# Windowed attention and its gated feed-forward: a first mask part of 32 rows, ten trios in the written-out start-up instead of twelve, and a new table

## The chip, the cores and the metric

The kernel runs on one core of a Trainium2 chip. The metric is device time in microseconds (us). The time before is 901.32 us, the median of three runs (901.23 to 902.42).

Five engines take part, each with an instruction queue of its own that it works through in order: TensorE (PE in the profile, its weight loads PEld) multiplies and transposes into PSUM; VectorE (DVE) and ScalarE (ACT) work element by element; GpSimd (POOL) takes over one subtraction per trio in the later part; SyncE (SP) issues nearly all loads. ACT issues the stores.

## The reference

```python
scores = scale * q @ k.T                      # 8 batches, 8 heads, 576 positions, 64 dims
mask: heads 0-3: 0 <= rel < 32;  heads 4-7: 0 <= rel < 128 and rel % 4 == 0
attn = softmax(where(mask, scores, -1e9));  x = attn @ v    # x: 4608 tokens x 512
h = x @ w_in                                  # 512 x 2048
g = h * clip(h + 3, 0, 6) / 6
out = g @ w_out                               # 2048 x 512
```

## The kernel before, in words

**Attention in trios.** Attention is cut into 48 trios, six per batch: four heads (kind 0 are the heads with the plain window, kind 1 those with the dilated one, whose positions are reordered by residue) times a third of the positions. One trio is 12 blocks of 32 queries for each of two pairs of heads. `block(ts, tv)` (line 262) issues the 48 small score products of trio `ts` and the 48 small value products of trio `tv`, interleaved; either may be left out. The first NFIRST = 12 trios ("masked", line 266) get their mask on PE: line 269 multiplies a unit matrix with the mask columns into the PSUM bank before the scores are added to it. Later trios get it on DVE, by an addition at line 221 in `largest`.

A trio's chain is: scores on PE; `largest` (line 215, a reduction) and `shifted` (line 227, a subtraction) on DVE; `exponent` (line 237) on ACT; a transpose; values on PE; `normalise` (line 240, three DVE instructions); a transpose back; then `high` (line 353, ACT rounds to fp32r) and `low` (line 360, the rest of it), which write the columns of `xh` and `xl` that the feed-forward reads. The first trios are transposed on PE, with a copy from PSUM by ACT (`turn_e`, `turned_e`, `turn_x`, `turned_x`, lines 292 to 315). The later ones go through `turn_by_blocks` (line 317): two transposes of 32 by 32 blocks on DVE, then four DMAs of 24 KB on SP. Their low part is made on POOL (`st_split`, line 367).

**Feed-forward in steps.** The tokens are 12 chunks of 384, the hidden width 16 slices of 128: 192 steps. Step n has a first product G (`gemm1`, line 448: 12 matmuls of 384 columns), the gate (`relu` on ACT, `gate` on DVE, `gate_high` on ACT, `gate_low` on DVE, lines 463 to 476), and a second product H (`gemm2`, line 478: nine matmuls of 512 columns, kept in three PSUM banks over a chunk). Every product is done in three parts, high by high, high by low, low by high. The list `steps` (line 374) starts with LEAD = 2 slices of chunk 0, then alternates between chunks 0 and 1, since each weight slice is fresh; from chunk 2 on it goes chunk by chunk. G of a chunk reads all trios that wrote its tokens: chunk 0 needs trios 0 to 4, chunk 1 trios 5 to 9 and earlier ones, chunk 2 (steps 32 on) trios 10 and 11 too.

**Weights.** Each of the 32 weight parts (two per slice) is loaded as 64-bit floats and converted: `U` and `Q` on ACT, `s`, `j`, `a` on DVE, `h` on ACT, `l` on DVE (lines 403 to 442).

**Order.** The start-up is written out in the table ORDER (line 40). Each word is an operation and a number, and every engine takes its own instructions in the order of the words. `k`, `v`, `w`, `M` load keys and queries, values, a weight part, a part of the mask; `B` is a block of scores with the values of trio number minus FOLLOW (3), `V` values alone; `R`, `S`, `X` are largest, shifted, exponent; `E`, `CA` the transpose and its copy; `Z` normalise; `Y`, `CX` the transpose back and its copy; `XH`, `XL` high and low part (on DVE here); `G`, `RE`, `T`, `GH`, `GL`, `H` the step. A word such as `k6@S2` is a load that SP issues only after S2 has ended. The old table holds 28 steps.

Behind the table, `step_at` (line 547) writes a step as G, the gate, what `beside` holds for its first half, H of two steps earlier (LAG), what `beside` holds for its second half. `place(p, ...)` (line 535) puts a part of a later trio at half-step p, counted from the start of chunk 2 (step 32), so that p = -1 is the second half of step 31. PE's order is this program order; DVE, ACT, SP and POOL are ordered by a scheduler there, in which a gate ranks above what lies beside its step. A trio takes four places: values of it and scores of the next at p, the transpose back at p + 1, the next one's transpose at p + 2, the split at p + 4. Below, "B10" and "V10" of a late trio mean its scores or values alone, and "G32" the G of step 32.

**Mask.** `mi` (line 125) holds a 128 by 128 unit matrix and the mask's six 384-column patterns; each pattern's 32 rows are repeated four times over the 128 partitions (`_mask`, line 597). It is loaded in two parts by columns (`load_mask`, line 502), and behind the first DVE copies the unit matrix to fp32 for the transposes (line 506).

Of the kernel before, what the change touches and what calls it, by code (L numbers as in the profile page):

```python
# [49 lines left out]
RE25 a5 s11 h5 T25 l5 w14@T20 G11 GH20 j11 GH25 a23 Q3 a11 h23 G6 Q14 l23 h11 U14 l11 w25@h5 U15 s14 H7 j14 Q25 s15  # L50
a14 H8 j15 RE11 RE6 T11 h14 T6 a15 H13 GH11 GL20 h15 l14 w2@U15 GH6 l15 w18@H8 Q2 G12 U2 GL25 GL11 U3 GL6 Q18 s2 s3
G17 U18 j2 RE12 j3 U19 T12 H20 a2 RE17 a3 h2 T17 h3 l2 H2 GH17 l3 w6@h15 GH12 Q6 s19 s18 U6 j19 G5 GL12 GL17 s6 a19
G1 RE5 j6 h19 T5 a6 GH5 H17 l19 w7@l15 Q7 h6 j18 U7 l6 w16@h19 H12 s7 RE1 GL5 Q16 T1 U16 j7 GH1 G9 s16 U17 GL1 a7
# [625 lines left out]
```

## Time and profile before

| | |
|---|---|
| runs | 901.23, 901.32, 902.42 us |
| the profiled execution | 901.94 us, of which 900.2 us are the span of the trace |
| PE busy | 881.0 us (98%) |
| PEld, DVE, ACT, POOL busy | 788.8, 450.0, 346.2, 43.3 us |
| start of the first step (G8) | 44.62 us |
| granted clock | full, but for two stretches between 22 and 34 us |

Matmuls are pipelined: the duration of one (0.34 us for 384 columns) is longer than the distance from one start to the next (0.17), and a group of instructions is best timed from its first start to the next group's first start. An idle time in square brackets at the end of a row is the engine's idle time just before the instruction, with what ended it; "issue" means that nothing in the profile accounts for it. [...]

### The profile page before, as it was taken

The numbers are of one execution on the slowest core, as the hardware profiler recorded it, in microseconds if no ns is written. First come the engines' busy times: TensorE is split into PE (matmuls) and PEld (weight loads), VectorE is DVE, ScalarE is ACT, GpSimd is POOL, SyncE is SP. The second block draws the span as 40 slices with busy tenths as digits, with TensorE's granted clock in tenths as the row PEclk, the third lists the DMA queues.
The fourth block names the chain that finished last, engine by engine and source line by source line (L and its number), as shares of the span: only waits on it lengthen the run. The fifth ranks groups of instructions, "written<-read, shape, count | busy, mean of one in ns | idle before, by whom it ended". The sixth has DMA issues, their size and how long they took to land.

```text
span 900.2 us, 20593 instructions
## 1 busy us (share of the span) xinstructions
PE 881.0 (98%) x8732; PEld 788.8 (88%) x8732; DVE 450.0 (50%) x952; ACT 346.2 (38%) x661; POOL 43.3 (5%) x59
## 2 busy tenths in 40 slices
...
DMA packets 37819, 74.86 MB, mean 83 GB/s; under 512 B 7264, under 2 KB 16608, under 8 KB 37728
## 3 DMA queue, kind: packets, MB, share of 16 engines
...
## 4 chain that ended last, share of the span: by engine, by line
PE 94%; DMA 2%; SPq 1%; ACT 1%; issue 1%; DVE 1%; ACTq 0%; DVEq 0%
PE ps_o L489 15%; PE ps_h L457 15%; PE ps_h L459 14%; PE ps_h L458 14%; PE ps_o L491 14%; PE ps_o L490 14%; PE ps_a L210 3%; PE ps_a L192 2%; PE ps_a L202 1%; PE ps_a L295 1%; DMA mi<-in_mask 1%; SPq L329 1%; DMA a<-a_t 1%; DMA first<-in_v 1%; ACT a L308 0%
## 5 line engine op out<-in xcount | busy, mean ns | idle before, releaser
L457 PE MATMUL ps_h<-xh,wt 128*128 128x384 f32 x768 | 260.6, 339 | 0.0
L468 DVE SCALAR_TENSOR_TENSOR t<-t,ps_h 128x384 f32<-128x384 f32 x192 | 106.1, 554 | 307.4 <-ACT t L465 307.2
L459 PE MATMUL ps_h<-xh,wt 128*128 128x384 f32 x768 | 258.5, 337 | 0.0
L458 PE MATMUL ps_h<-xl,wt 128*128 128x384 f32 x768 | 258.5, 337 | 0.0
L489 PE MATMUL ps_o<-wt,gh 128*128 128x512 f32 x576 | 228.4, 397 | 0.0
L491 PE MATMUL ps_o<-wt,gl 128*128 128x512 f32 x576 | 224.9, 390 | 0.0
L490 PE MATMUL ps_o<-wt,gh 128*128 128x512 f32 x576 | 224.4, 390 | 0.0
L465 ACT ACTIVATE t<-ps_h,three 128x384 f32<-128x384 f32 x192 | 110.8, 578 | 277.8 <-PE ps_h L459 271.9
L476 DVE TENSOR_TENSOR gl<-t,gh 128x384 fp32r<-128x384 f32 x192 | 106.5, 558 | 100.3 <-ACT gh L472 98.6
L457 PEld LDWEIGHTS ps_h<-xh,wt 128*128 128x128 f32 x768 | 144.6, 188 | 7.3
L458 PEld LDWEIGHTS ps_h<-xl,wt 128*128 128x128 f32 x768 | 144.7, 188 | 6.7
L459 PEld LDWEIGHTS ps_h<-xh,wt 128*128 128x128 f32 x768 | 144.7, 188 | 0.0
L472 ACT CAST gh<-t 128x384 fp32r<-128x384 f32 x192 | 98.0, 513 | 101.2 <-DVE t L468 97.3
L491 PEld LDWEIGHTS ps_o<-wt,gl 128*128 128x128 f32 x576 | 108.1, 188 | 23.2
L489 PEld LDWEIGHTS ps_o<-wt,gh 128*128 128x128 f32 x576 | 108.2, 188 | 18.4
L490 PEld LDWEIGHTS ps_o<-wt,gh 128*128 128x128 f32 x576 | 108.3, 188 | 15.9
L362 POOL TENSOR_TENSOR xl<-xf,xh 128x384 fp32r<-128x384 f32 (+3 forms) x54 | 43.0, 806 | 746.9 <-ACT xh L357 714.0
L238 ACT ACTIVATE e<-e 128x384 f32<-128x384 f32 x48 | 25.2, 525 | 105.7 <-DVE e L229 105.7
L192 PE MATMUL ps_a<-kq 64*32 64x64 f32 x1872 | 46.7, 226 | 0.0
L357 ACT CAST xh<-xf 128x384 fp32r<-128x384 f32 (+3 forms) x72 | 33.7, 535 | 32.4 <-DMA xf<-xf_t 32.2
L210 PEld LDWEIGHTS ps_a<-v,a 64*32 64x32 f32 x1728 | 35.8, 105 | 10.9 <-issue 9.2
L210 PE MATMUL ps_a<-v,a 64*32 64x65 f32 x1728 | 42.1, 225 | 1.0 <-DMA a<-a_t 1.0
...
## 6 DMA issues: line engine op xcount, KB each, us to landing
...
kq<-in_qk SPq DMA_DIRECT2D x39, 416.0 KB, 4.6
...
first<-in_qk SPq DMA_DIRECT2D x9, 416.0 KB, 5.3
...
```

The costliest lines, as they stand in the source:

```text
L192: return nc.tensor.matmul(ps[at : at + QB, 2 * QB * i : 2 * QB * (i + 1)], lhsT=x[rows, KW + QB * n : KW + QB * (n + 1)], rhs=x[rows, QB * ...
L210: return nc.tensor.matmul(ps[at : at + QB, i * W : (i + 1) * W], lhsT=ats[t][rows, QB * n : QB * (n + 1)], rhs=vs[t][rows, n, :], start=Tr ...
L457: nc.tensor.matmul(ph, lhsT=wt[f][:, 0, ks], rhs=a, start=(kt == 0), stop=False)
L458: nc.tensor.matmul(ph, lhsT=wt[f][:, 0, ks], rhs=b, start=False, stop=False)
L459: ins = nc.tensor.matmul(ph, lhsT=wt[f][:, 1, ks], rhs=a, start=False, stop=(kt == NK - 1))
L465: return nc.scalar.activation(ts[n], phs[n], AF.Relu, bias=three, scale=1.0)
L468: return nc.vector.scalar_tensor_tensor(out=ts[n], in0=ts[n], scalar=6.0, in1=phs.pop(n), op0=ALU.min, op1=ALU.mult)
L472: return nc.scalar.copy(ghs[n], ts[n])
L476: return nc.vector.tensor_tensor(out=gls[n], in0=ts.pop(n), in1=ghs[n].bitcast(F32), op=ALU.subtract)
L489: nc.tensor.matmul(po[c][tt], lhsT=gh[:, rows], rhs=wt[f][:, 2], start=first, stop=False)
L490: nc.tensor.matmul(po[c][tt], lhsT=gh[:, rows], rhs=wt[f][:, 3], start=False, stop=False)
L491: ins = nc.tensor.matmul(po[c][tt], lhsT=gl[:, rows], rhs=wt[f][:, 2], start=False, stop=(f == NF - 1))
```

## The change

The mask table gets a second unit matrix: a 32 by 32 one, repeated four times side by side (and on all four groups of rows). A product of its first 32 rows with the first 32 rows of a mask pattern repeats the pattern on all 128 partitions of PSUM. So line 269 now reads 32 partitions of the mask only, and the load is cut differently: M0 is rows 0 to 31 with all columns, M1 the unit matrix of the other 96 rows (256 bytes each), M2 the mask of these rows, which only the late trios read. The copy of the unit matrix to fp32 follows when M0 and M1 are both issued.

Ten trios instead of twelve stand in the table. Trios 10 and 11 become late ones: their scores at half-steps -10 and -9, transposes one half-step later, values at -7 and -5 (trio 12's scores with the latter), transposes back at -6 and -4, splits at -3 and -1; trio 12's own transpose stays behind, at -3. FOLLOW becomes a dictionary: seven blocks carry values, three trios' values go alone. LEAD = 6 puts six slices of chunk 0 ahead. The output scaling and the stores leave `gemm2` for a function of their own, `store`, with the word `O`. The table is new as a whole and has 27 steps, G20 first; most of its loads are let out by an `@`.

```diff
-LEAD = 2
-NFIRST = 12
+LEAD = 6
+NFIRST = 10
+NLATE = 12
-FOLLOW = 3
+FOLLOW = {2: 0, 3: 1, 4: 2, 5: 3, 7: 5, 8: 6, 9: 7}
 ORDER = """
-k2 k0 v0 M0 k9 M1 k4 k3 k1 w4 B0 R0 B2 S0 X0 E0 R2 CA0 v3@R2 S2 B3 X2 k6@S2 v6@X2 E2 Z0 B1 Q4 v2@E2 CA2 R3 U4 S3
-v1@R3 s4 X3 w10@s4 j4 Y0 R1 E3 CX0 k5@Y0 a4 CA3 XH0 S1 B6 v5@CA3 h4 XL0 X1 l4 v9@XL0 E1 w0@B6 Z3 CA1 R6 B4 S6 Q10 X6
-Y3 Z1 U10 B5 k7@Y3 CX3 R4 XH3 s10 S4 XL3 X4 j10 Y1 a10 E4 w1@B5 CX1 E6 Z2 CA4 XH1 R5 Y2 CA6 XL1 U0 B9 v4@CA6 S5 CX2
-s0 Q0 k11@CX2 j0 XH2 X5 Z6 v10@XH2 Q1 E5 XL2 h10 Y6 CA5 R9 CX6 k8@CA5 B7 a0 U1 S9 v8@a0 XH6 l10 X9 v7@XH6 XL6 h0 E9
-Z4 CA9 k10@E9 V9 R7 l0 Y4 B8 Z9 CX4 XH4 S7 s1 X7 XL4 Y9 Z5 w23@B8 E7 CX9 G8 CA7 R8 XH9 j1 XL9 Y5 RE8 S8 B10 w15@XL9
-CX5 a1 X8 w22@CX5 T8 XH5 E8 h1 Z7 G0 CA8 v11@h1 GH8 XL5 Q23 R10 w8@XL5 GL8 Y7 RE0 S10 B11 w29@Y7 CX7 l1 X10 T0 XH7
...
+k0 k1 M0 k2 k3 M1 w4 v0 v1 v3 B1 B0 R1 S1 R0 X1 S0 E1 X0 CA1 E0 w28@E0 Q4 CA0 U4 B2 k4@CA0 s4 j4 w26@s4 B3 R2 Z0
+v2@j4 S2 a4 X2 Q28 h4 k5@Q28 E2 U28 l4 Y0 CA2 v5@U28 R3 CX0 Z1 Q26 XH0 S3 Y1 U26 XL0 X3 s26 CX1 B4 s28 XH1 j26
+v4@s28 XL1 E3 a26 w2@XL1 CA3 R4 h26 B5 Z2 S4 k6@Z2 l26 X4 Y2 v6@S4 j28 E4 CX2 Z3 w0@E4 CA4 XH2 V4 R5 Q2 XL2 k7@XH2
+Y3 U2 Z4 CX3 v7@U2 B6 XH3 S5 s2 X5 Y4 XL3 k9@s2 E5 CX4 R6 XH4 j2 CA5 XL4 Q0 B7 k8@CA5 S6 U0 a2 X6 v8@U0 s0 E6 h2 Z5
+G20 w31@s0 CA6 R7 l2 S7 Y5 RE20 B8 j0 CX5 T20 X7 a0 XH5 E7 w1@X7 GH20 a28 G1 h0 XL5 CA7 Z6 h28 Q31 R8 B9 v9@Q31 RE1
+l0 Q1 S8 U1 GL20 Y6 G0 R9 X8 CX6 Z7 w6@R9 XH6 S9 XL6 Y7 X9 w3@G0 E8 T1 RE0 E9 s1 CX7 G2 T0 CA9 w27@CX7 j1 XH7 CA8
+l28 GH0 XL7 V9 GH1 RE2 a1 V8 Q3 Z9 h1 G22 w18@Q3 Z8 U3 Q6 l1 U6 GL0 Y9 Q27 w7@G22 s3 Y8 CX9 GL1 H0 CX8 j3 XH9 T2 XH8
+XL9 w9@XH9 GH2 XL8 RE22 a3 Q18 G7 Q7 GL2 T22 h3 w14@Q7 s6 U18 l3 G9 GH22 j6 RE7 Q9 GL22 U7 T7 a6 U27 H1 GH7 s18 s7
...
+w19@a10 Q8 a11 U8 T19 H18 h11 s8 GH19 l11 RE24 GL19 Q19 T24 G17 U19 j8 GH24 s19 U9 a8 H19 j19 h8 RE17 GL24 l8
+w20@l11 Q20 a19 U20 G4 T17 h19 s20 GH17 l19 j20 w21@l19 H12 RE4 GL17 a20 T4 h20 H17 s9 GH4 l20 GL4 Q21 j9 U21 G26 a9
+s21 h9 j21 G5 l9 w22@l20 RE26 a21 Q22 U22 T26 h21 s22 H4 GH26 l21 RE5 GL26 w23@l21 k10 k11 k12 v10 v11 v12 M2 T5 G14
+j22 GH5 GL5 a22 h22 H5 RE14 l22 Q23 T14 U23 G16 GH14 s23 GL14 j23 a23 H14 RE16 h23 T16 l23 GH16 G15 GL16 H16 RE15
+T15 GH15 G23 GL15 H24 RE23 T23 GH23 H15 GL23 O24 H23
 """
@@ -123,7 +123,8 @@
     xl = const.tile([P, NK, 2 * S], F32R, name="xl")
     mi = const.tile([P, mask.shape[1]], BF16, name="mi")
     ident_b = mi[:, :P]
-    mask_sb = mi[:, P:].rearrange("p (t x) -> p t x", t=6)
+    spread = mi[:QB, P : 2 * P]
+    mask_sb = mi[:, 2 * P :].rearrange("p (t x) -> p t x", t=6)
     ident = const.tile([P, P], F32, name="ident")
     three = const.tile([P, 1], F32, name="three")
@@ -266,7 +267,7 @@
         masked = ts is not None and ts < NFIRST
         if masked:
             _, kind, part = trios[ts]
-            nc.tensor.matmul(ps[:, :CH], lhsT=ident_b, rhs=mask_sb[:, 3 * kind + part], start=True, stop=False)
+            nc.tensor.matmul(ps[:, :CH], lhsT=spread, rhs=mask_sb[:QB, 3 * kind + part], start=True, stop=False)
         for i, u, r in blocks():
             if tv is not None:
                 product = (mm_values_first if tv < NFIRST else mm_values)(tv, pv, i, u, r)
@@ -482,27 +483,37 @@
         first = c not in po
         if first:
             po[c] = [ps_a.tile([P, DM], F32, name="ps_o", tag="ps_a") for _ in range(TT)]
-        if f == NF - 1:
-            o = wpool.tile([P, TT, DM], F32, name="o", tag="w")
         for tt in range(TT):
             rows = slice(tt * P, (tt + 1) * P)
             nc.tensor.matmul(po[c][tt], lhsT=gh[:, rows], rhs=wt[f][:, 2], start=first, stop=False)
             nc.tensor.matmul(po[c][tt], lhsT=gh[:, rows], rhs=wt[f][:, 3], start=False, stop=False)
             ins = nc.tensor.matmul(po[c][tt], lhsT=gl[:, rows], rhs=wt[f][:, 2], start=False, stop=(f == NF - 1))
-            if f == NF - 1:
+        done.add(n)
+        return ins
+    def store(n):
+        c, f = steps[n]
+        if f == NF - 1:
+            o = wpool.tile([P, TT, DM], F32, name="o", tag="w")
+            for tt in range(TT):
                 nc.scalar.mul(o[:, tt], po[c][tt], 1.0 / 6.0)
                 r = c * CH + tt * P
                 nc.scalar.dma_start(out=out[r : r + P, :], in_=o[:, tt])
-        done.add(n)
-        return ins
-    parts_of_mask = [0, P + 2 * CH, mask.shape[1]]
+    parts_of_mask = [
+        (slice(0, QB), slice(0, mask.shape[1])), (slice(QB, P), slice(0, P)), (slice(QB, P), slice(2 * P, mask.shape[1]))
+    ]
+    loaded = set()
     def load_mask(i):
-        cols = slice(parts_of_mask[i], parts_of_mask[i + 1])
-        ins = nc.sync.dma_start(out=mi[:, cols], in_=mask[:, cols])
-        if i == 0:
+        rows, cols = parts_of_mask[i]
+        ins = nc.sync.dma_start(out=mi[rows, cols], in_=mask[rows, cols])
+        loaded.add(i)
+        if loaded == {0, 1}:
             nc.vector.tensor_copy(out=ident, in_=ident_b)
         return ins
@@ -511,7 +522,7 @@
         "M": load_mask, "k": load_qk, "v": load_v, "w": load_w,
-        "B": lambda t: block(t, t - FOLLOW if t >= FOLLOW else None),
+        "B": lambda t: block(t, FOLLOW.get(t)),
         "V": lambda t: block(None, t),
         "R": largest, "S": shifted, "X": exponent,
         "E": turn_e, "CA": turned_e,
@@ -521,22 +532,29 @@
         "U": cv_product, "Q": cv_round, "s": cv_shift, "j": cv_sign, "a": cv_add, "h": cv_high, "l": cv_low,
-        "G": gemm1, "RE": relu, "T": gate, "GH": gate_high, "GL": gate_low, "H": gemm2,
+        "G": gemm1, "RE": relu, "T": gate, "GH": gate_high, "GL": gate_low, "H": gemm2, "O": store,
     }
     beside = {}
     halves = [(c, f, k) for c in range(2, NCH) for f in range(NF) for k in range(2)]
     at = [1 + 19 * i // 3 for i in range(10)]
-    at += [at[-1] + 8 * (i + 1) for i in range(T - NFIRST - 10)]
+    at += [at[-1] + 8 * (i + 1) for i in range(T - NLATE - 10)]
     place = lambda p, step: beside.setdefault(halves[p] if p >= 0 else (1, NF + p // 2, p % 2), []).append(step)
-    place(-3, lambda: st_both(NFIRST, None))
-    place(-1, lambda: ats.update({NFIRST: turn_by_blocks(es.pop(NFIRST), "a")}))
+    turned = lambda t: lambda: ats.update({t: turn_by_blocks(es.pop(t), "a")})
+    for i, t in enumerate(range(NFIRST, NLATE)):
+        place(i - 10, lambda t=t: st_both(t, None))
+        place(i - 9, turned(t))
+        place(2 * i - 7, lambda t=t: st_both(t + 1 if t + 1 == NLATE else None, t))
+        place(2 * i - 6, lambda t=t: xfs.update({t: turn_by_blocks(xs.pop(t), "xf")}))
+        place(2 * i - 3, lambda t=t: st_split(t))
+    place(-3, turned(NLATE))
     for i, p in enumerate(at):
-        t = NFIRST + i
+        t = NLATE + i
         more = t + 1 < T
         place(p, lambda t=t, more=more: st_both(t + 1 if more else None, t))
         place(p + 1, lambda t=t: xfs.update({t: turn_by_blocks(xs.pop(t), "xf")}))
@@ -557,6 +575,7 @@
         turn_of(n + G2)
         if n - LAG not in done:
             gemm2(n - LAG)
+            store(n - LAG)
         turn_of(n + DEL + 0.5)
         for step in beside.get((c, f, 1), []):
             step()
@@ -611,7 +630,8 @@
             full[kind, i] = np.where(ok, 0.0, NEG)
     m = np.stack([full[kind, 6 * part : 6 * part + 6].swapaxes(0, 1) for kind in range(2) for part in range(3)], axis=1)
     m = np.tile(m.reshape(QB, -1), (4, 1))
-    return np.concatenate([np.eye(P, dtype=np.float32), m], axis=1)
+    ones = np.eye(P, dtype=np.float32), np.tile(np.eye(QB, dtype=np.float32), (4, 4))
+    return np.concatenate([*ones, m], axis=1)
 def _by_residue(a):
```

## Rows read from the trace of the kernel before

**Rows 1.** Busy by stretch: PE, PEld, DVE, ACT, POOL, clock, DMA share, GB/s

```profile
20.00:30.00 10.00, 5.97 (x221) 4.38 (x213) 7.05 (x17) 4.25 (x9) 0.00 (x0) 0.83 0.81 308
30.00:40.00 10.00, 7.49 (x217) 6.18 (x215) 8.68 (x22) 8.55 (x19) 0.00 (x0) 0.83 0.74 232
...
200.00:300.00 100.00, 99.29 (x1131) 89.00 (x1130) 51.08 (x113) 33.20 (x65) 8.10 (x11) 1.00 0.27 81
```

**Rows 2.** PE timeline at the first step: start us, us, engine line op

```profile
44.62 0.42 PE L457 MATMUL ps_h<-xh,wt 128*128 128x384 f32 x1
```

**Rows 3.** PE's waits: us in total, times, longest us

```profile
PE ps_a L202 <- issue: 4.5, 3, 2.4
...
PE ps_a L210 <- DMA a<-a_t: 1.0, 2, 0.7
```

**Rows 4.** DMA issues at 2.2 and 2.6 us: count, KB, us to landing

```profile
mi<-in_mask SPq DMA_DIRECT2D x1, 224.0 KB, 6.2
...
kq<-in_qk SPq DMA_DIRECT2D x1, 416.0 KB, 6.8
```

**Rows 5.** Timeline of DVE in the start-up

```profile
10.38 0.56 DVE L225 TENSOR_REDUCE mx<-ps_a 128x6 f32<-128x384 f32 x1 [1.80 <-PE ps_a L192]
...
24.72 0.17 DVE L243 TENSOR_SCALAR z<-ps_a 128x6 f32<-128x6 f32 x1 [0.92 <-PE ps_a L202]
...
25.62 0.55 DVE L225 TENSOR_REDUCE mx<-ps_a 128x6 f32<-128x384 f32 x1
26.08 0.42 DVE L415 TENSOR_SCALAR st<-st 128x512 uint32<-128x512 uint32 x1
...
26.88 0.91 DVE L362 TENSOR_TENSOR xl<-xf,xh 128x192 fp32r<-128x192 f32 x2
27.70 0.69 DVE L421 SCALAR_TENSOR_TENSOR st<-st 128x512 uint32<-128x512 uint32 x1
```

**Rows 6.** Timeline of PE, first matmuls of G, H and the next G

```profile
164.44 0.34 PE L457 MATMUL ps_h<-xh,wt 128*128 128x384 f32 x1
...
166.53 0.39 PE L489 MATMUL ps_o<-wt,gh 128*128 128x512 f32 x1
...
168.57 0.34 PE L457 MATMUL ps_h<-xh,wt 128*128 128x384 f32 x1
```

**Rows 7.** Timeline of PE: trio 12's scores alone, and a later whole block

```profile
176.91 0.88 PE L192 MATMUL ps_a<-kq 64*32 64x64 f32 x48
177.72 0.45 PE L457 MATMUL ps_h<-xh,wt 128*128 128x384 f32 x1
...
215.18 0.24 PE L210 MATMUL ps_a<-v,a 64*32 64x65 f32 x1
...
216.28 0.45 PE L457 MATMUL ps_h<-xh,wt 128*128 128x384 f32 x1
```

**Rows 8.** Timeline, trio 12 from its exponent to its values

```profile
179.63 0.53 ACT L238 ACTIVATE e<-e 128x384 f32<-128x384 f32 x1 [1.83 <-DVE e L229]
...
182.33 0.37 DVE L325 STREAM_TRANSPOSE a_t<-e 128x192 f32<-128x192 f32 x1
...
186.17 0.24 PE L210 MATMUL ps_a<-v,a 64*32 64x65 f32 x1
...
186.96 0.24 PE L210 MATMUL ps_a<-v,a 64*32 64x65 f32 x1 [0.26 <-DMA a<-a_t]
```

**Rows 9.** Timeline, trio 12 from its values to its low part

```profile
187.96 0.45 PE L457 MATMUL ps_h<-xh,wt 128*128 128x384 f32 x1
...
192.96 0.37 DVE L325 STREAM_TRANSPOSE xf_t<-x 128x192 f32<-128x192 f32 x1
...
197.55 0.51 ACT L357 CAST xh<-xf 128x384 fp32r<-128x384 f32 x1 [1.34 <-DMA xf<-xf_t]
...
198.14 1.02 POOL L362 TENSOR_TENSOR xl<-xf,xh 128x384 fp32r<-128x384 f32 x1 [197.31 <-ACT xh L357]
```

**Rows 10.** Busy time in a stretch behind the first step, columns as above

```profile
50.00:90.00 40.00, 40.00 (x392) 36.80 (x392) 36.84 (x77) 34.56 (x69) 0.00 (x0) 1.00 0.59 196
```

More of the change, by code (lines that the diff above doesn't have):

```diff
@@ L45 @@
-Z4 CA9 k10@E9 V9 R7 l0 Y4 B8 Z9 CX4 XH4 S7 s1 X7 XL4 Y9 Z5 w23@B8 E7 CX9 G8 CA7 R8 XH9 j1 XL9 Y5 RE8 S8 B10 w15@XL9
-CX5 a1 X8 w22@CX5 T8 XH5 E8 h1 Z7 G0 CA8 v11@h1 GH8 XL5 Q23 R10 w8@XL5 GL8 Y7 RE0 S10 B11 w29@Y7 CX7 l1 X10 T0 XH7
-w17@X10 E10 Z8 GH0 G2 CA10 Q15 XL7 Q22 R11 U22 GL0 Y8 w19@G2 V10 RE2 S11 CX8 s22 H0 T2 X11 XH8 Z10 GH2 XL8 Q8 Y10
-GL2 U8 E11 j22 CX10 G13 CA11 s8 XH10 a22 Q17 XL10 Q29 j8 V11 w5@G13 RE13 a8 h22 G7 Q19 Z11 h8 T13 U23 l8 Y11 GH13 G3
-RE7 l22 CX11 w11@l8 GL13 Q5 T7 XH11 s23 G20 GH7 XL11 RE3 GL7 U5 T3 j23 GH3 G25 Q11 s5 GL3 RE20 w3@Q11 j5 U11 T20 H3
@@ L50 @@
[L50 to L53, printed above, removed]
-j16 h7 G4 s17 RE9 l7 w28@l19 T9 a16 Q28 H5 j17 RE4 h16 a18 U28 T4 h18 H25 l16 w9@l7 GH4 a17 GH9 s28 Q9 l18 U9 G19
@@ L55 @@
-j28 h17 U29 GL4 GL9 s9 G21 l17 w20@l16 Q20 RE19 j9 U20 T19 a9 H4 GH19 a28 h9 s29 h28 l9 w21@l17 G16 Q21 l28 RE21
-GL19 U21 j29 T21 H11 RE16 a29 s20 h29 T16 l29 w12@H4 Q12 G26 U12 j20 GH16 s12 GH21 a20 j12 G14 h20 s21 a12 l20 h12
-H19 j21 l12 w30@l29 a21 H6 h21 GL16 GL21 RE26 l21 RE14 T26 H16 T14 w13@H6 GH26 GH14 Q30 U30 G15 GL26 GL14 s30 Q13
-j30 U13 G23 a30 RE15 s13 h30 T15 l30 w31@GH26 Q31 H14 RE23 j13 U31 T23 a13 G18 GH15 s31 GH23 j31 h13 a31 G10 l13 h31
-l31 w26@l30 Q26 U26 H9 s26 j26 a26 H21 h26 GL23 GL15 RE18 l26 w27@s26 RE10 T18 H15 T10 GH18 Q27 GL18 U27 GH10 G24
@@ L60 @@
-s27 GL10 j27 a27 H18 RE24 h27 T24 l27 w24@RE10 k12 k13 k14 v12 v13 v14 Q24 GH24 H23 U24 GL24 s24 U25 j24 H10 s25 a24
-j25 h24 l24 H24 a25 h25 l25 G22 G27 RE22 T22 GH22 H1 GL22 RE27 T27 GH27 H22 GL27
+k0 k1 M0 k2 k3 M1 w4 v0 v1 v3 B1 B0 R1 S1 R0 X1 S0 E1 X0 CA1 E0 w28@E0 Q4 CA0 U4 B2 k4@CA0 s4 j4 w26@s4 B3 R2 Z0
+v2@j4 S2 a4 X2 Q28 h4 k5@Q28 E2 U28 l4 Y0 CA2 v5@U28 R3 CX0 Z1 Q26 XH0 S3 Y1 U26 XL0 X3 s26 CX1 B4 s28 XH1 j26
+v4@s28 XL1 E3 a26 w2@XL1 CA3 R4 h26 B5 Z2 S4 k6@Z2 l26 X4 Y2 v6@S4 j28 E4 CX2 Z3 w0@E4 CA4 XH2 V4 R5 Q2 XL2 k7@XH2
@@ new lines @@
+Q14 GL7 h6 j18 H7 U14 l6 w17@GH7 RE9 s14 T9 j14 G3 GH9 Q17 a18 a14 h18 GL9 h14 G11 l18 w29@a18 RE3 l14 T3 w30@l14 j7
+H9 GH3 RE11 s27 Q29 GL3 a7 U29 G8 T11 h7 j27 GH11 Q30 l7 w15@GH11 U30 GL11 H3 RE8 a27 U31 s29 T8 h27 j29 GH8 G12 Q15
+l27 w16@a27 U15 GL8 a29 H20 s15 h29 s31 RE12 j15 Q16 T12 U16 a15 G21 GH12 s16 U17 GL12 h15 j16 G25 l15 w5@U15 RE21
+a16 T21 h16 s17 GH21 H8 l16 j17 l29 w24@RE21 G10 a17 RE25 GL21 Q5 T25 h17 j31 GH25 H21 U5 l17 w25@l16 Q24 a31 Q25 s5
+s30 h31 H22 j5 RE10 U24 GL25 T10 U25 a5 G13 GH10 l31 h5 GL10 l5 w12@l17 Q12 U12 H10 s24 RE13 s12 j24 j12 H2 T13 a12
```

2 lines of the change are left out of this document (added).

## The prediction

> **What bounds the kernel now.** The views were read from coarse to fine. Equal stretches come first [rows 1]: from 200 to 300 us TensorE (PE) is busy 99.3 us of 100, VectorE (DVE) half of the time, and the granted clock is full. Only in the start-up does PE stand idle; 20 to 40 us shows it at 6.0 and 7.5 of 10 us, with a granted clock of 0.83 as well. So what can be won lies ahead of the first hidden-layer step (G8), which starts at 44.62 us [rows 2]. From there PE hardly pauses, and the end is that start plus PE's work. PE's waits [rows 3] are all small: 4.5 us in three stops that the profile gives to nobody ("issue"), and 1.0 us late, on a trio turned by DMA. In the start-up DVE is nearest to being the limit: it works from 10.38 us on, and its order is written out.
>
> Sums are made against the profiled execution, 901.94 us (span 900.2); the median of the runs is 0.62 below it and is what I forecast. A measurement tells about 0.2% (1.8 us) from no change.
>
> **The mask and the first reduction.** The first part is now 32 rows (164 KB) behind two key loads, not 224 KB behind two and a value load; it landed at 2.12 + 6.2 = 8.3 us [rows 4]. The next load, with which 1.86 MB of the queue had gone, landed at 2.59 + 6.8 = 9.4. That is 1.1 us for 0.42 MB; taken back from 1.45 MB to the 1.0 MB that now go up to M0, it lands near 7, and at full use of the queue ahead of it near 6. So PE may start 1 to 2 us earlier. But DVE's first item is the copy of the unit matrix, which now waits for M0 and M1, and M1 stands behind two more key loads: 1.85 MB, hence 9.4 again. With 0.25 us for the copy the first reduction starts at 9.7 instead of 10.38 [rows 5]: only 0.7 us. The 32-row product costs PE what the 128-row one did (384 columns either way); bounds are nothing and its double, off the limit here. The last part (M2, 442 KB) goes to the table's end on SP, behind one weight load and six trio loads; some 18 us of listed PE work lie between that place and trio 10's scores, and 3.4 MB at the 0.4 MB/us of those landings take 9: nothing.
>
> **The new table up to its first step (G20).** I counted DVE's entries ahead of the scores that precede G20 (through S6): 7 reductions at 0.46, 7 subtractions and 4 shifts (one of each takes 0.80: 0.46 and 0.34), 5 normalisations at 0.90, 5 low parts (two at 0.46, three in two pieces at 0.82), and 8 further conversion entries, busy 0.69 each and overlapping to some 0.62 [rows 5]: 20.6 us. The same count ahead of G8 in the old table gives 26.2: nine reductions stand there, seven here. The old waits of DVE are 44.62 - 10.38 - 26.2 = 8.0. In the new table, following the listed order, 4.2 of waits come out whatever the loads do: 2.7 after S0, where the next entry is a conversion that ACT only reaches behind exponent, transpose and copy of trio 0 (four links of nearly 0.6), 1.0 ahead of the first weight's addition, 0.5 elsewhere. Exponent and transpose after S6 add 1.1. Without disturbance G20 starts at 9.7 + 20.6 + 4.2 + 1.1 = 35.6. [...] Bounds are nothing, and all 8.0 of the old waits in place of 4.2 (35.6 to 39.4). I take 2.0, because fewer small products precede G20 and DVE has up to about 1 us of slack at each block: **G20 at 37.6, 7.0 earlier**.
>
> [...]
>
> **PE's work behind it.** A step is 2.09 (first product) and 2.04 (second) [rows 6]; 192 of each remain in both kernels. Transposes and blocks listed behind the first step are 7.6 us in the old table (as timed) and 7.4 by count in the new one: equal. The masks and transposes saved for trios 10 and 11 lie ahead of it and are in the 7.0. Added are three lone late blocks, B10, B11 and V10, at 0.81, and V11 beside B12 instead of B12 alone (1.10 for 0.81) [rows 7]: 3 x 0.81 + 0.29 = **+2.7**. Six steps ahead instead of two only reorders steps. The output scaling, now an entry of its own (three on ACT with three DMAs), is covered by some 6 us of PE work before B10 needs the bank; uncovered it would cost one scaling, 0.6.
>
> **The two late trios.** They are now turned by DVE and four DMAs each on SP, in steps 27 to 31, ahead of chunk 2, whose first product (G32) reads both. Trio 12 shows the chain today [rows 8]: its scores end at 177.72, the exponent at 180.16, DVE turns it from 182.33 (behind a gate), its values, begun at 186.17, go on at 186.96: 9.2 us, 7.1 without the hold. V10 has H25, B11, G28, H26 ahead of it, 7.0 us. Wait 0.1 to 2.2; with the gates of step 27 and the three DVE entries of trio 11's scores in the way, **+1.3**. The second chain, from values to low part [rows 9]: the block ends at 187.96, DVE turns from 192.96 (behind the next trio's scores and a gate), ACT splits at 197.55, POOL ends at 199.16: 11.2 us. Trio 11's runs the same course, DVE's work on trio 12's scores included, and PE has only two steps, 8.3 us, before G32. Less 0.4 for an output scaling that stood in the way then: bounds 0.6 (turned 2 us earlier) and 2.9, taken **+2.6**. What is queued behind it is everything, since PE runs in order. In return B12 now comes six half-steps ahead of its values, and the old wait there (186.17 to 187.96 is 1.79, for a block of 1.10) goes: **-0.7**.
>
> **DVE behind G20.** From G20 to H8 PE has 48.1 us listed and DVE 47.1, of which DVE begins 1.1 earlier; at G7 the margin is nil. DVE idles 3.2 us in 40 today [rows 10], harmless because the old table's margin grows to 2 us by G3. Bounds: nothing, and all the idling, 3.8. **+0.9**, as most falls where a margin of 0.5 to 2 is left.
>
> Sum: -7.0 + 2.7 + 1.3 + 2.6 - 0.7 + 0.9 = -0.2 on 901.94; on the median **901.1 us**: no change that a measurement tells.
>
> **Rivals.** *The late trios are hidden.* If the order on DVE lets the transposes go ahead of gates, both waits fall to their lower bounds (0.1 and 0.6): 3.2 less, 897.9. For it: 2 us of both old chains are holds, not work. Against: both old chains show the hold.
> *The start-up runs as listed*, G20 at 35.6: 899.1. For it: loads are let out fewer at a time than before; against: the stops.
> *DVE becomes the limit between G20 and H8* (the other side): each stop of DVE for another engine passes to PE, 3.8 instead of 0.9: 904.0. It decides the sign from 2.9 us of passed-on idling (903.1). For it: the margins above; against: the idling of rows 10 was seen with DVE off the limit.
> *The start-up loses what it lost before*, G20 at 39.4: 902.9; the change's earlier mask would then do nothing.
> *The clock.* At 20 to 40 us the granted clock averaged 0.83 [rows 1], after PE had stood idle; G32's wait is a gap of that kind. The two drops there lost 0.17 of 20 us, 1.7 each; one such behind G32's wait gives 902.8. [...]
>
> **How the numbers follow.** Forecast 0.40 (0.28 within 0.2%, 0.06 on each side), late trios hidden 0.16 (faster), start-up as listed 0.12 (0.09 faster, 0.03 same), DVE the limit 0.18 (slower), start-up as before 0.08 (0.05 same, 0.03 slower), clock 0.06 (0.04 same, 0.02 slower). Faster 0.31, same 0.40, slower 0.29. Range: at the lower end hidden trios with G20 at 36 (897.9 - 1.6 = 896.3), at the upper DVE's limit with one more of 1.8 (905.8).
>
> **What would show it.** Right: the first reduction near 9.7, G20 near 37.6, a wait of 1 to 2 us at V10, about 2.6 us of PE at G32 for POOL's low part of trio 11, no wait at V12. Wrong: G20 before 36 or after 40; G32 without a wait; PE waiting for DVE in the 40 us behind G20 by more than 2.9 us in all; the first reduction near 8, which would say that M1 does not wait its turn.

## The result, and the profile after

The changed kernel took **905.84 us** (median of 5 runs, 904.92 to 907.92) beside 901.32 for the kernel before, run beside it (5 runs, 900.98 to 904.89): ratio 1.0048 [1.0026, 1.0069], slower by more than the 0.2% that can be told. The forecast was 901.1, no change, with 905.8 as the upper end of the range; the measured time lies just outside it. The profiled execution took 906.40 (span 904.6, before 900.2).

The forecast named signs of being right or wrong; the views below answer them. The waits of PE in the changed kernel (us in total, times, longest us; they answer to [rows 3]):

```profile
PE ps_h L458 <- ACT xh L358: 3.1, 1, 3.1
...
PE idle L137 <- DVE zeros L134: 1.3, 1, 1.3
```

The "issue" stops of 4.5 us are gone, the wait at the head of the program (1.3 us for DVE's zeros) is the old one, and a wait of 3.1 us, longer than any of those stops (2.4 at most), stands late, where the kernel before had nothing over 0.7: G32 waits for the high part of trio 11. Busy time by stretch (columns as in [rows 1], the clock as a share of the full one):

```profile
20.00:30.00 10.00, 8.12 (x206) 6.01 (x206) 9.17 (x23) 5.62 (x13) 0.00 (x0) 0.52 0.80 251
30.00:40.00 10.00, 8.12 (x214) 6.63 (x215) 8.41 (x21) 8.24 (x18) 0.00 (x0) 0.79 0.81 255
180.00:190.00 10.00, 6.52 (x21) 5.44 (x20) 2.19 (x6) 1.57 (x4) 0.99 (x1) 0.72 0.11 30
```

PE is busier in the start-up than before, at a lower clock, and there is a new hole: 6.5 of 10 us at 180, with the granted clock at 0.72 (0.50, the half clock, from 186 to 190). The timeline of PE at the first step, at trio 10's values and at G32 (start us, us, engine line op):

```profile
38.68 0.42 PE L458 MATMUL ps_h<-xh,wt 128*128 128x384 f32 x1
...
165.90 0.30 PE L211 MATMUL ps_a<-v,a 64*32 64x65 f32 x2
166.40 0.30 PE L211 MATMUL ps_a<-v,a 64*32 64x65 f32 x4 [0.20 <-DMA a<-a_t]
166.98 0.87 PE L211 MATMUL ps_a<-v,a 64*32 64x65 f32 x42 [0.27 <-DMA a<-a_t]
167.78 0.44 PE L458 MATMUL ps_h<-xh,wt 128*128 128x384 f32 x1
...
173.21 0.44 PE L458 MATMUL ps_h<-xh,wt 128*128 128x384 f32 x1
...
181.36 0.39 PE L490 MATMUL ps_o<-wt,gl 128*128 128x512 f32 x1
184.85 0.69 PE L458 MATMUL ps_h<-xh,wt 128*128 128x384 f32 x1 [3.09 <-ACT xh L358]
185.92 0.69 PE L459 MATMUL ps_h<-xl,wt 128*128 128x384 f32 x1 [0.38 <-POOL xl L363]
...
188.00 0.53 PE L459 MATMUL ps_h<-xl,wt 128*128 128x384 f32 x1
...
192.19 0.39 PE L490 MATMUL ps_o<-wt,gl 128*128 128x512 f32 x1
```

G20 begins at 38.68, 5.94 us earlier than G8 did [rows 2]. The block of trio 10's values lasts 1.88 us (165.90 to 167.78) instead of 0.80; that of trio 11's values and trio 12's scores ends at 173.21, where G30 begins. From the last matmul of H29 (181.36) to the last of H30 (192.19) pass 10.83 us; the matmuls of G32 last 0.53 where the same form lasts 0.34 at full clock [rows 6]. The trio behind that wait, on DVE and ACT:

```profile
9.49 0.23 DVE L517 CAST ident<-mi 128x128 f32<-128x128 bf16 x1 [8.22 <-DMA mi<-in_mask]
9.63 0.55 DVE L226 TENSOR_REDUCE mx<-ps_a 128x6 f32<-128x384 f32 x1
...
173.73 0.56 DVE L247 TENSOR_TENSOR x<-ps_a,z 128x384 f32<-128x384 f32 x1
...
179.06 0.66 DVE L477 TENSOR_TENSOR gl<-t,gh 128x384 fp32r<-128x384 f32 x1 [2.27 <-ACT gh L473]
179.65 0.37 DVE L326 STREAM_TRANSPOSE xf_t<-x 128x192 f32<-128x192 f32 x1
...
177.68 0.52 ACT L358 CAST xh<-xf 128x384 fp32r<-128x384 f32 x1 [1.48 <-DMA xf<-xf_t]
178.10 0.53 ACT L239 ACTIVATE e<-e 128x384 f32<-128x384 f32 x1
178.53 0.50 ACT L473 CAST gh<-t 128x384 fp32r<-128x384 f32 x1
...
184.28 0.51 ACT L358 CAST xh<-xf 128x384 fp32r<-128x384 f32 x1 [2.10 <-DMA xf<-xf_t]
```

Trio 11's output is multiplied at 173.73 and transposed from 179.65. In between, on ACT, the high part of trio 10 (XH10, 177.68) waits 1.48 us for its DMAs with the gate's high part GH30 (178.53) behind it; DVE waits 2.27 for GH30, and the transposes stand behind that. Trio 12's transposes in the kernel before stood behind a gate too, but DVE waited 0.90 us for it there:

```profile
192.49 0.56 DVE L476 TENSOR_TENSOR gl<-t,gh 128x384 fp32r<-128x384 f32 x1 [0.90 <-ACT gh L472]
```

The mask's parts, issued at 1.64 and 3.05 us (count, KB, us to landing):

```profile
mi<-in_mask SPq DMA_DIRECT2D x1, 160.0 KB, 4.8
mi<-in_mask SPq DMA_DIRECT2D x1, 24.0 KB, 6.3
```

The 32 rows are there at 6.5, and still the first reduction comes at 9.63, behind the copy of the unit matrix that needs the second part at 9.4.

### The profile page after: what moved, and what is told of

Its sections match the earlier page's. It is cut to its first block, busy times and chain, and to the rows that moved or that the text cites. A ratio compares the mean times of both kernels' runs of the same rounds, so it can differ in the third digit from the quotient of the medians.

```text
span 904.6 us, 20609 instructions
## 1 busy us (share of the span) xinstructions
PE 886.0 (98%) x8718; PEld 790.5 (87%) x8718; DVE 451.7 (50%) x960; ACT 343.9 (38%) x657; POOL 45.4 (5%) x61
## 4 chain that ended last, share of the span: by engine, by line
PE 92%; DMA 2%; DVE 2%; ACT 2%; SPq 1%; issue 1%; POOL 0%; DVEq 0%; ACTq 0%
PE ps_o L488 15%; PE ps_h L458 14%; PE ps_h L459 14%; PE ps_h L460 14%; PE ps_o L490 14%; PE ps_o L489 14%; PE ps_a L211 3%; PE ps_a L193 2%; PE ps_a L203 1%; SPq L330 1%; PE ps_a L296 1%; DMA mi<-in_mask 1%; DMA a<-a_t 1%; DMA st<-in_w 0%; DMA xf<-xf_t 0%
## 5 line engine op out<-in xcount | busy, mean ns | idle before, releaser
L363 POOL TENSOR_TENSOR xl<-xf,xh 128x384 fp32r<-128x384 f32 (+3 forms) x56 | 45.1, 816 | 749.6 <-ACT xh L358 700.8
L211 PEld LDWEIGHTS ps_a<-v,a 64*32 64x32 f32 x1824 | 37.6, 105 | 11.6 <-issue 9.6
L211 PE MATMUL ps_a<-v,a 64*32 64x65 f32 x1824 | 44.3, 225 | 0.8 <-DMA a<-a_t 0.8
```

The source lines that it names most:

```text
L211: return nc.tensor.matmul(ps[at : at + QB, i * W : (i + 1) * W], lhsT=ats[t][rows, QB * n : QB * (n + 1)], rhs=vs[t][rows, n, :], start=Tr ...
```

## The experiments

All times are medians. The kernel before ran beside each of them on the same chip (901.4 to 901.9); ratios and their intervals are to it, and kernels that did not run side by side are best compared by these ratios. Theory A: the loss is G32's wait with the half clock behind it. Theory D: it lies in the start-up. Theories A2 to A4 below say what makes the wait.

**The splits placed later.** `place(2 * i - 3, split)` became `place(-1, split)` for trios 10 and 11.

> The splits of trios 10 and 11 are placed two halves later (both at the last place), so that the ACT copy of trio 10 (XH10), which stood waiting 1.48 us for its DMAs in the changed kernel, no longer stands ahead of GH30 on ACT. Theory A (the loss is G32's wait for trio 11, 3.3 us with the low part's 1 us behind it, and the half clock behind that, 3.4 us; the wait is so long because XH10 holds GH30, GL30 and with them the transposes of trio 11's x): the wait in front of G32 shrinks by 1 to 2 us to about 1.5 to 2.3, the transposes of trio 11's x start at about 178 instead of 179.65, and the run comes out 1 to 2 us shorter where the clock still falls, 4 to 5 us where it does not: 901 to 905. Theory B (the chain of trio 11 itself, block to transposes to DMAs to copies, is too long and ACT's order does not matter): the wait stays 3.0 or more and the time stays at 905.8 within 1. Theory C (the loss is in the table's start at half clock and nothing at G32 counts, since PE is held later anyway): G32's wait shrinks, the time does not.

905.95 us (6 runs), 1.0045 [1.0027, 1.0063]; G32 waits 3.2. The edit decided nothing: in its trace XH10 stands ahead of GH30 as before, and around G32 the order is the same on every engine. It is the changed kernel a second time. Its first G came at 36.77, 1.91 earlier than in the first trace, and its profiled time was 904.29, 2.11 less: the start-up varies by that much from one execution to the next and the end follows it.

**Work in G32's wait.** Ahead of `gemm1`'s matmuls, for G32 alone (the products are overwritten):

```
+        for _ in range(18 if (c, f) == (2, 0) else 0):
+            nc.tensor.matmul(ph, lhsT=wt[f][:, 0, :P], rhs=xh[:, 0, CH : 2 * CH], start=True, stop=True)
```

> 18 more matmuls of 384 columns stand on PE ahead of G32, into G32's own PSUM bank, and are overwritten by G32's first: they fill the wait with work (about 18 x 0.17 = 3.1 us) and change nothing else. Theory A, its second half (the clock fell to half for 6.8 us because PE stood idle in that wait, which cost 3.4 us): the granted clock stays at full in 180 to 195, G32 takes 2.2 instead of 4.75, H30 2.0 instead of 2.9, and the run comes out 3 to 3.5 us shorter at about 902.4, with G32's start where it was, within 0.3. Rival (the clock falls for another reason, or the lost time is given back later by other waits): half clock stays, or it goes and the time stays at 905.8; 0 to 0.5 us longer where the extra matmuls outlast the wait.

905.39 us (10 runs), 1.0040 [1.0027, 1.0054]: the clock held and the trace was shorter behind G32, but the run with the splits placed later, in effect the changed kernel, took 905.95 beside it. A gain of 0.6 us is far from the 3 to 3.5 expected and is not told from nothing. So the changed kernel and the filled one were run once more, side by side:

> The changed kernel once more, unaltered, to have its time and a second trace beside the other runs of this call. Theory: 905 to 907, G32 again waits 2.9 to 3.6 us and the clock falls to half behind it; the first G lies between 36 and 39, and that difference is found again in the span. Rival (the first trace's wait of 3.1 us was a chance of that execution): the wait is under 2 us.

> The kernel with 18 more matmuls ahead of G32 once more. Its trace had shown 2.3 us less between the ninth G of the first chunks and the twenty-ninth than the changed kernel's, its times only 0.5 to 0.7 us less. Theory A, second half (the half clock behind the wait costs 2 us here): again no half clock in 180 to 195, and the median is 1.5 to 2.5 us under that of the changed kernel in this call. Rival (the clock is given back by something else in most executions): under 0.8 us.

The changed kernel took 906.73 (5 runs), 1.0058 [1.0044, 1.0072], the filled one 904.65 (6 runs), 1.0033 [1.0021, 1.0044]: **2.1 us**, though G32's own matmuls begin at the same distance from H29's last one (3.87 us without the fillers, 3.85 with them). Stretches of the changed kernel here, with the last matmul of H29, the first of G32 and the last of H30:

```profile
180.00:190.00 10.00, 5.89 (x24) 4.94 (x23) 3.12 (x7) 2.19 (x5) 1.85 (x2) 0.88 0.25 84
...
182.53 0.39 PE L490 MATMUL ps_o<-wt,gl 128*128 128x512 f32 x1
186.40 0.44 PE L458 MATMUL ps_h<-xh,wt 128*128 128x384 f32 x1 [3.48 <-ACT xh L358]
...
192.91 0.40 PE L490 MATMUL ps_o<-wt,gl 128*128 128x512 f32 x1
```

and the same of the filled one:

```profile
180.00:190.00 10.00, 9.04 (x101) 7.72 (x103) 2.65 (x6) 2.12 (x4) 1.00 (x1) 1.00 0.09 24
...
180.35 0.39 PE L492 MATMUL ps_o<-wt,gl 128*128 128x512 f32 x1
...
184.20 0.44 PE L460 MATMUL ps_h<-xh,wt 128*128 128x384 f32 x1 [0.33 <-ACT xh L358]
...
189.12 0.39 PE L492 MATMUL ps_o<-wt,gl 128*128 128x512 f32 x1
```

The kernels differ in nothing but what PE does in the wait; with work in it the clock stays full. From H29's last matmul to H30's last pass 8.77 us instead of 10.38, 1.6 less; the first filled trace has 8.54 beside 10.83 in the changed kernel's first, 2.3 less. So the half clock costs some 2 us: 1.6 and 2.3 by the traces, 2.1 and 0.6 by the medians of the two pairs, where 3 to 3.5 were expected at first.

**One more step of work ahead of G32.** From G32 on, H follows its G by one step, not two, so that H30 stands ahead of G32:

```
+        if n == 2 * NF:
+            gemm2(n - LAG)
+            store(n - LAG)
...
-        if n - LAG not in done:
+        m = n - LAG if n < 2 * NF else n - 1
```

> From G32 on, H follows its G by one step instead of two: H30 stands ahead of G32 on PE, so that 2.04 us of work that was behind the wait fills it. Theory A: G32's wait falls from 3.3 to about 1.2 us, the low part's wait with it, and whether the clock falls shows whether a wait of this size triggers it; the run is 2 us shorter where it still falls, 5 us where not: 900.5 to 904. Rival (with a lag of one step the H of each later step waits for its own gate, relu to low part, about 3 us after G's end, under one G of 2.18 us and the steps' other work): each of some 190 later steps gains a wait of 0.2 to 1 us and the kernel is slower by 40 us or more.

903.63 us (12 runs), 1.0022 [1.0009, 1.0035]: 2.2 less than the first median of the changed kernel, as expected for a clock that still falls. The wait for xh fell to 1.4 us with 0.6 for the low part behind it, and the half clock came none the less (0.83 granted from 180 to 190 us); the feared wait of each later step did not come.

**The transposes at once.** `st_both` and the later `turn_by_blocks` of trios 10 and 11 become one step:

```
+    def st_late(ts, tv):
+        block(ts, tv)
+        normalise(tv)
+        xfs[tv] = turn_by_blocks(xs.pop(tv), "xf")
+        if ts is not None:
+            largest(ts), shifted(ts), exponent(ts)
```

> The two DVE transposes of the output of trios 10 and 11, and the four DMAs behind them, are issued right behind that output's multiplication instead of one half later; nothing else moves. In the changed kernel trio 11's output was there at 174.3 and its transposes began at 179.65, behind the scores of trio 12, the gate of step 30 and a wait for XH10. Theory A2 (G32's wait is made by where the transposes are placed, not by the length of the chain or by ACT's order, which the run with later splits left at 3.6 us): trio 11's transposes start 5 us earlier, its high part is on ACT by 180, G32 follows H29 with no wait, the clock stays at full in 180 to 195, G32 takes 2.2 and H30 2.0; together 3.3 for the wait, 0.9 for the low part and 2.3 to 3.4 for the clock: the run is 6 to 7.5 us shorter, 898.3 to 900. Rival A3 (the chain through DMAs is itself as long as the wait, whatever the place): the wait falls by under 1.5 us and the time stays above 904. Rival A4 (trio 12, whose reduction, exponent and transposes move 0.9 us back, is then what PE waits for): G32's wait goes, a wait of 1 us or more comes in front of the block that multiplies trio 12's values, and the run is 901 to 903.

**900.16 us** (12 runs), 0.9981 [0.9966, 0.9995]: 5.7 less than the changed kernel's first median and 6.6 less than its second. The timeline of its DVE, ACT and PE:

```profile
175.37 0.56 DVE L247 TENSOR_TENSOR x<-ps_a,z 128x384 f32<-128x384 f32 x1
175.96 0.38 DVE L326 STREAM_TRANSPOSE xf_t<-x 128x192 f32<-128x192 f32 x1
...
181.81 0.51 ACT L358 CAST xh<-xf 128x384 fp32r<-128x384 f32 x1 [1.23 <-DMA xf<-xf_t]
...
182.82 0.39 PE L490 MATMUL ps_o<-wt,gl 128*128 128x512 f32 x1
183.05 0.34 PE L458 MATMUL ps_h<-xh,wt 128*128 128x384 f32 x1
183.47 0.44 PE L459 MATMUL ps_h<-xl,wt 128*128 128x384 f32 x1
...
187.31 0.39 PE L490 MATMUL ps_o<-wt,gl 128*128 128x512 f32 x1
```

The transposes follow the output by 0.59 us instead of 5.92, G32 follows H29 without a wait, and from the last matmul of H29 to that of H30 pass 4.49 us instead of 10.83: 6.3 less. Theories A and A2 hold, at the lower end of the size expected (898.3 to 900); trio 12, moved back by the transposes, made PE wait nowhere. XH10 still waits in ACT's queue, now ahead of step 30's relu (177.97, behind an idle time of 4.66 us), but the transposes no longer stand behind a gate, and PE does not feel it.

**Trio 10's values one half later as well**: in the kernel just told, `place(2 * i - 7, st_late)` became `place(i - 6, st_late)`.

> As the run with the transposes at once, and the block that multiplies trio 10's values is put one half later (between the two halves where it stood and where trio 11's stands). Theory: its wait of 1.08 us for the DMAs of trio 10's weights goes (0.80 instead of 1.88 us), and with G32's wait gone as well the run is 1.1 us shorter than that with the transposes at once alone: 897.2 to 899. Rival: the wait returns in front of G32, since trio 10's output is split one half later: no gain against it, or up to 1 us of loss.

901.96 us (12 runs), 0.9999 [0.9987, 1.0011], 1.8 slower than without the move: the rival, by more than the 1 us it allowed. Trio 10's wait shrank to one of 0.24 us, and a wait of 0.9 us stood in front of G32 again, with the half clock behind it (0.83 from 180 to 190).

**XH10 alone.** A dependency puts the copy of trio 10's high part behind GH30; every other engine keeps the changed kernel's order:

```
+    def split_behind(t):
+        behind = last["activate"]
+        ins = high(t)
+        tc.add_manual_dep(ins.ins, behind, ...)
+        low(t, nc.gpsimd)
```

> The changed kernel with one instruction moved: the ACT copy of trio 10 (XH10) is held behind GH30 by a dependency, on ACT two places later; the order of every other engine stays. (The run with the splits placed two halves later had left every engine's order as it was, so this question was not put by it.) Theory A (XH10's wait for its DMAs, 1.5 to 1.6 us on ACT, holds GH30, with it GL30 on DVE and so the transposes of trio 11's output): these start 1.5 to 1.9 us earlier against the end of H28, G32's wait for trio 11's high part falls from 3.1 to 3.5 us to 1.4 to 2.0, and the run is 1.5 to 2 us shorter where the clock still falls behind it: 904 to 905.2. Rival A2 alone (only the place of the transposes behind trio 12's scores and the gate counts, 5 us, and ACT's order nothing): the wait stays above 2.7 and the time at 905.8 to 906.7.

**903.24 us** (12 runs), 1.0011 [1.0000, 1.0022]: one instruction two places later on an engine that is 38% busy is worth 2.6 to 3.5 us (against the two medians of the changed kernel, which did not run beside it; the intervals of the ratios lie apart), more than the 1.5 to 2 expected. Its timeline:

```profile
176.84 0.51 ACT L473 CAST gh<-t 128x384 fp32r<-128x384 f32 x1 [0.21 <-DVE t L469]
177.75 0.52 ACT L358 CAST xh<-xf 128x384 fp32r<-128x384 f32 x1 [0.39 <-DMA xf<-xf_t]
...
177.86 0.37 DVE L326 STREAM_TRANSPOSE xf_t<-x 128x192 f32<-128x192 f32 x1
...
182.51 0.51 ACT L358 CAST xh<-xf 128x384 fp32r<-128x384 f32 x1 [1.03 <-DMA xf<-xf_t]
...
183.07 0.45 PE L458 MATMUL ps_h<-xh,wt 128*128 128x384 f32 x1 [1.30 <-ACT xh L358]
```

The transposes begin 1.8 us earlier (177.86 instead of 179.65, with H28 ending at the same place) and G32's wait falls from 3.1 to 1.3. So 1.8 of it hang on ACT's order as long as the transposes stand behind the gate, and all of it goes when they don't, as the run before showed: the place of the transposes and the copy ahead of the gate made the wait together.

**Two queues.** The transposes at once, and in `turn_by_blocks`, for trios 10 and 11, `(nc.scalar if c > 1 and queues == 2 else nc.sync).dma_start(`.

> The transposes at once, and of the four DMAs that follow each of them for trios 10 and 11 two go through ACT's queue and two through SP's, where all went one behind the other through SP's (0.83 us each: eight in 6.64 us). Theory (the 1.08 us that the block of trio 10's values waits, and the 0.35 us for trio 11's low part, come from DMAs issued one behind the other): that block takes 0.80 to 1.2 instead of 1.88 us, and the run is 0.8 to 1.4 us shorter than with the transposes at once alone, 898.8 to 899.4. Rival (ACT, which then waits for DVE's transposes at the DMAs, holds relu and the high parts of the gates): a wait for relu or gate in front of a G or H in 160 to 185, time 900.5 to 903.

**899.63 us** (8 runs), 0.9974 [0.9961, 0.9988]. PE at trio 10's values, and SP's queue for its half of the DMAs of trio 10's weights:

```profile
165.75 1.03 PE L211 MATMUL ps_a<-v,a 64*32 64x65 f32 x48
166.71 0.44 PE L458 MATMUL ps_h<-xh,wt 128*128 128x384 f32 x1
...
163.10 1.47 SPq L330 DMA_DIRECT2D a<-a_t  x2
```

All four in the changed kernel:

```profile
163.25 2.49 SPq L330 DMA_DIRECT2D a<-a_t  x4
```

The block takes 0.96 instead of 1.88, as expected, and no wait of PE is left late. The expectation reads one row of eight DMAs in 6.64 us as eight in a row at 0.83; they are trio 10's four, 2.49 us, and trio 11's four from 167.2 on, after a pause for their transposes, and only the first four lie ahead of trio 10's values. Trio 10's are now issued within 1.5 us (SP's two from 163.10 to 164.57, ACT's two from 163.07 to 164.34) instead of 2.5, and here that lay on the path. In the time a gain over the transposes at once (900.16, 0.9981) is not shown: 0.5 us, inside both intervals, where 0.8 to 1.4 were expected.

**The start-up's clock.** 72 matmuls of the unit matrix by itself (product not used) in PE's gaps of the table: `B0 F16 R1`, `E1 F6`, `E0 F8`, `B3 F10`, `Y0 F32`; first in the changed kernel, then in the one with the transposes at once.

> 72 matmuls of the unit matrix by itself (128 columns, bf16, product not used) are put into PE's order in the first 30 us, where PE stood waiting in the changed kernel: 16 behind B0, 6 behind E1, 8 behind E0, 10 behind B3, 32 behind Y0. Theory D (the first step came at 38.7 and not at 37.6 or before because the start-up ran at half clock for 17.1 us, against 6.8 in the kernel before, PE's gaps being what dropped it): half clock in the first 39 us falls below 8 us, blocks go from 2.0 to 1.33 us, the first G comes 2 to 4 us earlier at 34.7 to 36.7, and the run is 2 to 4 us shorter at 902 to 904. Rival E (the start-up is bound by DVE and its exponents, PE's clock lies beside them): first G within 0.7 us of 38.7, time within 1 us of 905.8. Rival F (the fillers delay the chain where PE's gaps were shorter than they are): first G later by 1 to 3 us, time 907 to 909.

> The transposes at once (900.2), and the 72 matmuls of the unit matrix by itself in PE's gaps of the first 30 us (product not used), whose one trace had a stall of 2.6 us that the others lack. Theory D (half clock in the start-up costs time): 897.5 to 899.3, half clock in the first 40 us below 5 us and the first G at 35 to 37. Rival E (PE's clock lies beside DVE's work and the loads there): 899.8 to 900.8 and the first G at 36.5 to 39.3 as without them.

905.40 us (12 runs) and 899.92 (11 runs), against 905.84 to 906.73 and 900.16 without: at best a few tenths, which these runs don't tell from nothing. The one trace of the first has its first G at 40.75, behind an "issue" stop of 2.6 us; that of the second at 37.49, among those without fillers. Busy time of the first 40 us in the changed kernel's first trace:

```profile
0.00:40.00 40.00, 30.02 (x732) 21.25 (x733) 24.33 (x58) 20.21 (x41) 0.30 (x5) 0.79 0.80 261
```

in its second trace:

```profile
0.00:40.00 40.00, 29.46 (x728) 20.30 (x729) 24.44 (x58) 20.51 (x41) 0.30 (x5) 0.92 0.79 265
```

One program had 0.79 in one execution and 0.92 in another, and its first G at 38.68 and 38.83 (the second has "issue" stops of 1.7 us as well). The ten traces with this table show no relation either: at 0.70 the first G came at 38.95 and 39.29, at 0.96 at 39.28. Theory D, in the form that the half clock held G20 back, falls.

**The mask.** First the changed kernel with the mask loaded as before (all 128 rows, `lhsT=ident_b`, no third part); then with the second part ahead of two key loads (`k0 k1 M0 M1 k2 k3`); then the latter in the kernel with two queues.

> The changed kernel's table and everything else, but the mask is loaded as before: all 128 rows, first the unit matrix with the first two patterns, then the other four; the mask matmul takes the unit matrix of 128 rows, and there is no third load. Theory A (the 32-row load brings the first reduction forward by what it lands earlier): the first reduction, at 9.63 with 32 rows, comes at 10.4 to 11.2, and the first G 0.7 to 1.5 us later: 906.5 to 907.3. Rival (the start is set further back in the chain, by DVE and the weights, and the mask's 0.75 us are absorbed): first G within 0.7 us, which is what it moves from run to run, and the time within 0.8 us of 905.8.

> In the changed kernel's table the load of the other 96 rows of the unit matrix (the copy of which stood ahead of the first reduction on DVE, at 9.49) is issued right behind the first mask load, ahead of two loads of queries and keys. Theory D2 (the first reduction waits for that copy and the start hangs on the first reduction): the copy is done by 8.3, the first reduction starts at 8.3 to 8.5 instead of 9.63, and the first G comes 0.7 to 1.3 us earlier: 904.5 to 905.1. Rival (the start hangs on what follows, the third and fourth trios' queries and keys now land later): first reduction earlier, first G the same or up to 1 us later, time 905.3 to 907.

> The transposes at once and the DMAs through two queues (899.6), with the other 96 rows of the unit matrix loaded right behind the first mask part. Theory from the run with that load alone (first reduction 2.5 us earlier, time unchanged at 906.1): 899.0 to 900.2, no gain. Rival (there the late trios' wait swallowed it, and without that wait the earlier reduction shows): 897.5 to 898.8.

906.33 us (12 runs), 906.08 (12 runs) and 899.32 (9 runs, 0.9967 [0.9953, 0.9981]; without it 0.9974, inside that interval). DVE's first reduction with the whole mask:

```profile
8.19 0.56 DVE L226 TENSOR_REDUCE mx<-ps_a 128x6 f32<-128x384 f32 x1 [1.80 <-PE ps_a L193]
```

and DVE's start and the first G with the second part ahead of the key loads, in the changed kernel otherwise:

```profile
6.20 0.23 DVE L517 CAST ident<-mi 128x128 f32<-128x128 bf16 x1 [4.94 <-DMA mi<-in_mask]
7.17 0.56 DVE L226 TENSOR_REDUCE mx<-ps_a 128x6 f32<-128x384 f32 x1 [0.75 <-PE ps_a L193]
...
11.85 0.43 DVE L416 TENSOR_SCALAR st<-st 128x512 uint32<-128x512 uint32 x1 [2.46 <-ACT st L408]
...
34.35 0.42 PE L458 MATMUL ps_h<-xh,wt 128*128 128x384 f32 x1
```

The changed kernel has the same wait of DVE for ACT:

```profile
14.28 0.43 DVE L416 TENSOR_SCALAR st<-st 128x512 uint32<-128x512 uint32 x1 [2.45 <-ACT st L408]
```

Loading 32 rows first makes the first reduction later (9.63) than the whole mask does (8.19), as the copy waits for the rest. In the medians neither the whole mask nor the 2.46 us won by the earlier copy (7.17) makes a difference, though the intervals leave room for 1 to 2 us. The traces point the other way: DVE's wait for ACT is no longer than in the changed kernel, so that DVE stays 2.4 us ahead, and the first G comes at 34.35, 4.3 us earlier than in the changed kernel's first trace; with the whole mask it comes at 36.23. But each is one execution, the shortest of its twelve (903.15 and 903.77). In the six traces that keep G32's wait without fillers in it (the changed kernel's two, the splits placed later, the fillers in the start-up, and these two) the time is 867.5 to 868.8 us more than the start of the first G; by that, an estimate, the medians of 906.08 and 906.33 belong to a first G between 37.3 and 38.8, where the changed kernel's lies too. Whether an earlier first reduction brings G20 forward stays open.

## Why the prediction was wrong

It forecast no change, with a sum of -0.2; the two spans differ by +4.4.

- **The first reduction**, 9.7 forecast, 9.63 seen: right, with its reason (the copy behind M1). Whether it carries to G20 is not shown, as the mask runs tell. PE's own wait for the mask, which the prediction's account of PE's waits leaves out, fell from 3.5 us to 1.6. The 32-row mask product takes PE 0.33 us where the clock is full, as the 128-row one does.
- **G20 at 37.6, -7.0**: 38.68, -5.94. In the ten traces whose table is the changed one it lies between 36.8 and 39.3, 38.3 in the mean: the term was some 0.7 to 1.1 us too large, within what one kernel's executions differ by. Of its 2.0 us for disturbance, chosen because fewer small products precede G20, no run shows that stops come with small products: the changed kernel's first trace has no "issue" stop, its second 1.7 us of them. What holds G20 there is open; it is not the clock.
- **Late blocks +2.7**: right as far as the rows go; the scores of trios 10 and 11 stand alone at 0.80 each, and the blocks of trios 11 and 12 share one of 1.10 us.
- **V10's wait +1.3**: 1.08, about right; that its four DMAs one behind the other in one queue make the difference was not forecast.
- **G32's wait +2.6, bounds 0.6 and 2.9: the step that failed.** The stretch lost 6.3 against the kernel without the wait: G32 begins 3.3 later, the wait for the low part takes 0.6 more, and what follows is 2.4 slower at the half clock. The waiting alone, about 4, lies over the upper bound. The forecast took trio 11's chain to be 11.2 us as trio 12's was, less 0.4, against 8.3 of PE's work (which gives 2.5). PE's work was right (8.4, from 173.2 to H29's end at 181.6); the chain was 12.7 us, from the block's end (173.2) to the low part's end (185.9). All of the 1.5 over trio 12's chain lies ahead of its transposes: 6.4 us from the block's end to the first of them, 5.0 for trio 12 [rows 9]. DVE waits there 2.27 us for GH30, where it waited 0.90 for the gate ahead of trio 12's, because trio 10's copy stands in ACT's queue ahead of that gate, itself waiting for DMAs. A chain priced from a row brings the neighbours it had there, not those it will get.
- **The clock** was put beside the forecast as a rival of 0.06 with +1.7. It was a consequence of the forecast's own wait, not another case: behind waits of 3.1 and 3.5 us at G32 the granted clock was 0.72 and 0.88 from 180 to 190 us, and 1.00 with work in that wait. Its size was about right: some 2 us.
- **V12 -0.7 and DVE behind G20 +0.9**: the wait at trio 12's values went, as forecast; PE's waits for DVE in the 40 us behind G20 are 0.6 in all. The rival of DVE as the limit, which would have met the measured time nearly (904.0), is not what happened.

With -5.9, +2.7, +1.1, +6.3, -0.7 and +0.6 the named parts give +4.1 of the 4.4; smaller differences lie beside them. The -5.9 is the difference of two single traces and moves by a microsecond or two from one execution to the next.

The gain was there: with trios 10 and 11 transposed at once and two queues the same table runs at 899.6, 0.26% [0.12, 0.39] under the kernel before. How much of it the six steps of lead or the order of the table bring alone was not tried.
